# Zero products issued inside units, ahead of a product foreseen to wait, and a higher bound for those at units' ends

## The chip, the cores and the metric

One NeuronCore of a Trainium2 chip runs the whole kernel. The metric is the device time of one execution in microseconds; a lower one is better. In the profile, PE is the TensorE matmul, PEld its weight load, DVE the VectorE, ACT the ScalarE, POOL the GpSimd engine and SP the engine that issues DMAs.

## The reference

Four attention layers in a row, each with a layer norm before it and a residual added: A, B, A, B. There are 2048 tokens of width 512, and 32 heads of 16. Layer A cuts the sequence into 4 segments of 512, with causal attention inside each and a linear-attention memory carried from segment to segment; layer B is full attention without a mask.

```python
# layer A, for each of the 4 segments s
logits = jnp.einsum('bhqd,bhkd->bhqk', qs, ks) * scale + mask
p = _softmax(logits, axis=-1)
a_dot = jnp.einsum('bhqk,bhkd->bhqd', p, vs)
a_mem = num / den                      # phi(q) against the memory M, z
o = g * a_mem + (1.0 - g) * a_dot
# layer B
scores = jnp.einsum('bhqd,bhkd->bhqk', q, k) * Dh ** (-0.5)
p = _softmax(scores, axis=-1)
o = jnp.einsum('bhqk,bhkd->bhqd', p, v)
# the whole
x = x + _A_ref(_layernorm(x), ...); x = x + _B_ref(_layernorm(x), ...)   # twice
```

## The kernel before, in words

The work is cut into **units**. A unit takes up to three score banks: for three blocks of 128 keys of some head, TensorE multiplies keys by queries (`ps<-qm,KA`, `ps<-qm,KB` or `ps<-qm,QA`: K of 32 rows, so that four heads share the array, "row-shaped"), into PSUM. ACT turns them into exponentials `pT` (line 1644), two sets of banks taking turns. In layer A, POOL cuts the diagonal blocks to the causal half (line 1659). Two or three units later TensorE multiplies `pT` by the values into the **accumulator**, bank 7 (`ACC`). In one form the values stream through `pT` as weights (`ps<-VA,pT`, all 128 rows and columns, "full-shaped", 51 or 34 columns each); in the other (`ps<-pT,VB` and the like) `pT` streams through values of 17 columns ("narrow"). Each head's **group** has the accumulator to itself from its first value product to its last; then DVE divides by the row sums (`finish`). Some score blocks go to DVE and POOL, which work out the exponential by integer steps (`dxw`, lines 1185, 1255, 1300), to relieve ACT; their products read `dxw` or another tile that is free at that time. Projections of the neighbouring layers (`ps<-xT,wB`, `ps<-wA,xT`, `ps<-woB,oT` ...) are spread between the units.

The order of all this isn't written out: a planner (`Sched`) goes through the program once before it is built, adds each instruction to its engine's list, and estimates when it starts and ends (`estimate`; `t["pe"]` and `t["act"]` are the estimated times at which an engine is through with what it has). `attention` runs the loop over units; a table of numbers (`PIECES`) changes its rules as the estimated time goes by. Each engine works through its list in order and waits on semaphores only where the planner's dependencies ask for it.

**Zero products** are matmuls of a 128x128 tile of zeros (`zero`) by 512 columns of `wB`: they add zero, and are there to keep TensorE at work. `keep_busy` issues them at the end of each unit, into the open accumulator where the group has had a value product, else into bank 3. It has two rules. The first ("fill") enters its products into the planner's estimate. The second ("add") passes `extra`: `Sched.add` then leaves the estimate of every time as it is, and only notes the product in `true`, from which `worked` reads the share of a stretch of 3413 ns that TensorE's products fill. "add" goes on while this share, in the stretch that ends at the later of `t["pe"]` and `t["act"]` - 1330, is under `ADD`, to at most `ADDS` products in all.

Of the kernel before, what the change touches and what calls it, by code (L numbers as in the profile page):

```python
# [24 lines left out]
UNIT, DXB, ACC = (0, 4), 3, 7  # L25
# [3 lines left out]
LAG = {"pe": 100, "act": 60, "dve": 60, "pool": 70, "sp": 50}  # L29


class Op:
    __slots__ = ("eng", "idx", "fn", "deps", "emit", "evno", "is_dma", "batch", "name", "end")

    def __init__(self, eng, idx, fn, name=""):
        self.eng = eng
        self.idx = idx
        self.fn = fn
        self.deps = []
        self.emit = False  # L40
        self.evno = None
        self.is_dma = False
        self.batch = None
        self.name = name
        self.end = 0.0
# [35 lines left out]
class Sched:  # L81


    def __init__(self):
        self.ops = {e: [] for e in ENGS}
        self.t = {e: 0.0 for e in ENGS}
        self.tiles = []
        self.held = []

        self.streams = []  # L90
        self.true = []

    def streamed(self, until, ns):

        while self.streams and self.streams[0][0] < self.pe_issue() - 2 * ns:
            self.streams.pop(0)
        return sum(w for t, w in self.streams if t >= until - ns) / ns
# [47 lines left out]
    def add(self, eng, fn, reads=(), writes=(), deps=(), name="", banks=(), ns=300, gap=None, tile=None, extra=None):  # L145
        op = Op(eng, len(self.ops[eng]), fn, name)
        dep_ops = list(deps)
        for b in reads:
            if b.last_write is not None:
                dep_ops.append(b.last_write)  # L150
        for b in writes:
            if b.last_write is not None:
                dep_ops.append(b.last_write)
            dep_ops.extend(b.reads.values())
        for (bk, mode, alloc) in banks:
            if mode == "w":
                if bk.alloc != alloc:
                    tail = bk.writes[-1:] + list(bk.reads.values())
                    if not tail:
                        tail = list(bk.prev_tail)  # L160
                    dep_ops.extend(tail)
                    bk.prev_tail = tail
                    bk.alloc = alloc
                    bk.writes = []
                    bk.reads = {}
                    bk.last_read_any = None
                else:
                    dep_ops.extend(bk.reads.values())
                    if not bk.writes and not bk.reads:
                        dep_ops.extend(bk.prev_tail)  # L170
            else:
                assert bk.alloc == alloc, (bk.idx, bk.alloc, alloc, name)
                if bk.writes:
                    dep_ops.append(bk.writes[-1])
                else:
                    dep_ops.extend(bk.prev_tail)
                if bk.last_read_any is not None and bk.last_read_any.eng != eng:
                    dep_ops.append(bk.last_read_any)
        wit = {}
        for w in dep_ops:  # L180
            if w.eng == "pe" and eng == "pe" and not w.is_dma:
                continue
            if w.is_dma:
                wit[("dma", id(w.batch))] = w
                continue
            cur = wit.get(w.eng)
            if cur is None or cur.idx < w.idx:
                wit[w.eng] = w
        for w in wit.values():
            if not w.is_dma:  # L190
                w.emit = True
        op.deps = list(wit.values())
        if extra is not None:
            op.end = max([w.end for bk, mode, al in banks for w in bk.writes[-1:] or bk.prev_tail], default=0.0)
            self.true.append((extra, tile[5] / 2.4))
        else:
            self.estimate(op, ns, max(ns - 85, 60) if gap is None else gap, tile, name[:3] in ("dxs", "dxp"))
        for b in reads:
            b.reads[eng] = op
        for b in writes:  # L200
            b.last_write = op
            b.reads = {}
        for (bk, mode, alloc) in banks:
            if mode == "w":
                bk.writes.append(op)
            else:
                bk.reads[eng] = op
                bk.last_read_any = op
        self.ops[eng].append(op)
        return op  # L210
# [73 lines left out]
class Builder:  # L284
# [7 lines left out]
    DXA_N, DXA_W, APARTS, FILL_NEAR, FILL_FREE, HOR, PHI, QUAD = 13, ('k0', 'k13'), ('k2', 'k13', 'k0'), 0, 1, 400, 'kq', ('in', 1, 3)  # L292
    QREST, CLOSE, FM, NAREA, XDX, NEAR_S, NEAR_E, DX_WAIT = 24, ('proj', 2, 2), 3, 18, 99, 60, 60, 400
    DX_RES, CHAINS, ALT, ALTS, ALTA = 0, 4, 0, 3, (1, 1, 1, 1)
    PSH, PSH_N, PSH_B, PSH_E, TODO, ONE, MOST, FULLW, FULL_N, MIX, OPART, ADD, ADDS, ADD_A = 0, 12, 4, 0, 350, 0, 2, 1, 8, 0, 4, 0.5, 3, 1330
    ORDER = [[(-4.6, 7.7, 7.6, 0.9, -10), (3.8, -10.8, 0.4, 20, -10.8), (19, 59.6, 22, 59.8, 12), (31, 44.3, 46.9, 10.6, 0.2)],
             [(-1.5, -6.7, -5.8, 20.8, 1.2), (-5.2, -1.6, 28.5, 28, 7), (21, 35.0, 8.2, 30, 27.7), (21, 48.0, 37, 23.6, 12.2)]]
    PIECES = [(0.0, {'MIX': 0, 'OPART': 4}),
# [180 lines left out]
    def keep_busy(self):  # L479


        g, n = self.cur, 0
        own = g is not None and g.npv
        if not own and (self.bank_late() > 0 or any(t["next"][0][:1] == ["cont"] for t in self.tasks)):
            return
        bank, al = (self.banks[ACC], g.acc) if own else (self.banks[DXB], self.new_alloc())
        soon = [w.end + LAG[w.eng] for e in self.pvq[:9] if e[0] <= self.unit_no + 1 for w in (self.b_pT[e[4] * 3 + e[5]].last_write,)]
        at = max(self.sc.t["act"] - 1330, min(soon, default=0.0) - self.HOR)
        while n < self.FILLS and self.sc.streamed(max(self.sc.t["pe"], at), 3413) < self.FILL:
            self.mm(self.ps[:, bank.col0:bank.col0 + 512], self.zero[:, :], self.wB[:, 0, 0:512], not own, not own,  # L490
                    [self.b_zero, self.b_wB[0]], bank, al, "fill")
            n += 1
        at = max(self.sc.t["pe"], self.sc.t["act"] - self.ADD_A)
        while n < self.ADDS and self.sc.worked(at, 3413) < self.ADD:
            self.mm(self.ps[:, bank.col0:bank.col0 + 512], self.zero[:, :], self.wB[:, 0, 0:512], not own, not own,
                    [self.b_zero, self.b_wB[0]], bank, al, "add", extra=at - 1)
            n += 1

    def mm(self, out, lhsT, rhs, start, stop, reads, bank, alloc, name="", tile=(128, 0, 128, 0), n=512, on=None, extra=None):
# [1346 lines left out]
    def pv_close(self, g, must):  # L1846


        whole = lambda: g.npv == g.total and not any(t[1] is g for t in self.dxq) and not any(p["ents"][0][0] is g for p in self.pooled)
        if not whole():  # L1850
            self.pv_some(g, (), must)
            if must and any(p["ents"][0][0] is g for p in self.pooled):
                self.pool_feed(g)
                self.pv_some(g, (), True)
            while must and g.npv < g.total:
                self.forced += 1
                if any(e[0] is g for e in self.dx_build):
                    self.dx_close()
                if any(p["ents"][0][0] is g for p in self.pooled):
                    self.pool_feed(g)  # L1860
                    self.pv_some(g, (), True)
                    continue
                mine = [t for t, l in zip(self.dx_tasks, self.dx_now) if l and l[1][0][0] is g]
                self.forcing = True
                self.run(mine[0] if mine else self.dx_next())
                self.forcing = False
                self.pv_some(g, (), True)
            if not whole():
                return 0
        self.cur = self.pend = None  # L1870
        cost = self.finish(g)
        if g.last:
            self.nfin[(g.L, g.qseg)] = self.nfin.get((g.L, g.qseg), 0) + 1
            if self.nfin[(g.L, g.qseg)] == 8:
                self.flags.add(("attn", g.L, g.qseg))
        return cost
# [149 lines left out]
```

## Time and profile before

| what | value |
|---|---|
| median of 3 executions | 1755.17 us (1754.55 to 1759.04) |
| the profiled execution | 1755.03 us, its span 1753.0 us |
| busy: PE, ACT | 1586.9 us (91%), 1709.0 us (97%) |
| busy: DVE, POOL | 1489.3 us (85%), 650.2 us (37%) |
| mean granted TensorE clock | 0.998 |
| weight loads of `zero` | 190 |

The span runs from the first to the last instruction; the profiled execution's own time has 2.0 us more around it. Busy shares are means over stages with different limits, so the prediction reads single places: rows of the timeline have start, duration, engine, line, operation, tiles, shape and count, and in brackets the idle time before and what ended it. Neighbours of one kind are merged into one row with their count; a row's duration then runs from the first one's start to the last one's end. Nearly all products of TensorE are recorded on line 500, since the helper `mm` issues them.

### The profile page before, as it was taken

The numbers are of one execution on the slowest core, as the hardware profiler recorded it, in microseconds if no ns is written. First come the engines' busy times: TensorE is split into PE (matmuls) and PEld (weight loads), VectorE is DVE, ScalarE is ACT, GpSimd is POOL, SyncE is SP. The second block draws the span as 40 slices with busy tenths as digits, with TensorE's granted clock in tenths as the row PEclk, the third lists the DMA queues.
The fourth block names the chain that finished last, engine by engine and source line by source line (L and its number), as shares of the span: only waits on it lengthen the run. The fifth ranks groups of instructions, "written<-read, shape, count | busy, mean of one in ns | idle before, by whom it ended". The sixth has DMA issues, their size and how long they took to land.

```text
span 1753.0 us, 43708 instructions
## 1 busy us (share of the span) xinstructions
PE 1586.9 (91%) x17387; PEld 567.8 (32%) x17570; DVE 1489.3 (85%) x2912; ACT 1709.0 (97%) x1662; POOL 650.2 (37%) x1204
## 2 busy tenths in 40 slices
PE   7889898899898999989999989989899999999998
PEld 4445454453224222233222232242222222222222
DVE  6687867589986999887999879767999999999997
ACT  7999999999999999999999999999999999999998
POOL 4632415110016212234211252151155566666665
PEclk9999999999999999999999999999999999999999
DMA  6021101000001000010001010010000000000000
GB/s 175 20 48 31 32 17 26 14 12 5 13 1 26 1 1 13 13 20 8 13 8 23 10 23 16 13 26 13 1 13 1 2 7 8 1 1 13 1 1 13
DMA packets 86188, 30.08 MB, mean 17 GB/s; under 512 B 78816, under 2 KB 85472, under 8 KB 85984
## 3 DMA queue, kind: packets, MB, share of 16 engines
q1 hardware_dynamic: 85984, 27.29, 7.6%
q8 instruction: 137, 2.24, 0.6%
q14 instruction: 67, 0.55, 0.1%
HBM read 6.30 MB, written 2.10 MB: 5 GB/s over the span
## 4 chain that ended last, share of the span: by engine, by line
ACT 45%; PE 29%; issue 14%; DVE 9%; POOL 2%; DMA 1%; SPq 0%; ACTq 0%; DVEq 0%; POOLq 0%
ACT pT L1644 44%; PE ps L500 29%; POOL pT L1659 2%; DVE dxw L1185 1%; DMA xT<-xn 1%; DVE dxw L1255 1%; DVE QA L1185 1%; ACT amem L758 0%; DVE VA L1185 0%; DVE xT L1185 0%; DVE KB L1185 0%; DVE KA L1777 0%; DVE x L975 0%; DVE VB L538 0%; DVE lnst L643 0%
## 5 line engine op out<-in xcount | busy, mean ns | idle before, releaser
L1644 ACT ACTIVATE pT<-ps 128x1024 bf16<-128x1024 f32 (+4 forms) x1612 | 1677.2, 1184 | 29.3 <-PE ps L500 21.4
L500 PE MATMUL ps<-qm,KB 32*128 32x512 bf16 x3584 | 524.5, 385 | 68.1 <-ACT pT L1644 54.3
L500 PE MATMUL ps<-pT,VB 128*17 128x512 bf16 x2187 | 372.1, 385 | 9.7 <-ACT pT L1644 3.4
L1659 POOL TENSOR_SCALAR_AFFINE_SELECT pT<-pT 128x256 bf16<-128x256 bf16 (+2 forms) x523 | 212.3, 417 | 222.3 <-ACT pT L1644 209.4
L500 PEld LDWEIGHTS ps<-qm,KB 32*128 32x128 bf16 x3584 | 133.4, 91 | 462.8 <-ACT pT L1644 347.8
L1300 POOL TENSOR_TENSOR dxw<-dxw,dxc 128x256 int32<-128x256 int32 (+1 forms) x127 | 77.7, 614 | 391.3 <-DVE dxw L1185 76.2
L1185 DVE TENSOR_SCALAR dxw<-ps 128x512 uint16<-128x512 f32 (+1 forms) x232 | 158.5, 697 | 5.2 <-PE ps L500 4.2
L500 PEld LDWEIGHTS ps<-pT,VB 128*17 128x17 bf16 x2187 | 86.6, 87 | 233.3 <-issue 199.4
L1554 POOL TENSOR_SCALAR qm<-QB,par 128x512 bf16<-128x512 bf16 x88 | 67.4, 772 | 246.5 <-PE ps L500 221.7
L1185 DVE TENSOR_SCALAR QA<-ps 128x512 uint16<-128x512 f32 (+1 forms) x170 | 120.7, 729 | 5.2 <-PE ps L500 4.5
L500 PE MATMUL ps<-qm,KA 32*128 32x384 bf16 (+3 forms) x1024 | 101.5, 303 | 24.7 <-ACT pT L1644 19.8
L500 PE MATMUL ps<-qm,QA 32*128 32x512 bf16 x512 | 113.1, 384 | 11.7 <-ACT pT L1644 8.3
L500 PE MATMUL ps<-VA,pT 128*128 128x51 bf16 (+1 forms) x2560 | 107.1, 187 | 16.7 <-POOL pT L1659 8.2
L500 PE MATMUL ps<-dxw,VW 128*17 128x512 bf16 x472 | 117.9, 383 | 0.0
L1185 DVE TENSOR_SCALAR VA<-ps 128x512 uint16<-128x512 f32 (+1 forms) x149 | 107.1, 732 | 4.7 <-PE ps L500 3.7
L1255 DVE TENSOR_SCALAR dxw<-dxw 128x1024 uint16<-128x1024 uint16 (+1 forms) x261 | 104.8, 412 | 4.5 <-PE ps L500 2.3
L500 PEld LDWEIGHTS ps<-VA,pT 128*128 128x128 bf16 x2560 | 84.4, 96 | 64.3 <-POOL pT L1659 31.7
L1185 DVE TENSOR_SCALAR KB<-ps 128x512 uint16<-128x512 f32 (+1 forms) x122 | 93.8, 786 | 4.5 <-PE ps L500 3.5
L500 PE MATMUL ps<-dxw,VB 128*17 128x512 bf16 x297 | 89.5, 382 | 0.1
L1185 DVE TENSOR_SCALAR VB<-ps 128x512 uint16<-128x512 f32 (+1 forms) x106 | 82.7, 794 | 3.6 <-PE ps L500 2.5
L500 PE MATMUL ps<-pT,VA 128*17 128x512 bf16 x367 | 74.7, 384 | 1.3 <-ACT pT L1644 1.1
L500 PE MATMUL ps<-VB,pT 128*128 128x34 bf16 (+1 forms) x1788 | 69.3, 186 | 2.0 <-ACT pT L1644 1.1
(343 smaller groups left out, 2782.9 us busy)
## 6 DMA issues: line engine op xcount, KB each, us to landing
out_dram<-x SPq DMA_DIRECT2D x8, 256.0 KB, 2.2
x<-in_A_x_dram SPq DMA_DIRECT2D x3, 512.0 KB, 5.1
wB<-in_B_wqkv_dram SPq DMA_DIRECT2D x1, 1536.0 KB, 11.8
xT<-xn SPq DMA_TRANSPOSE x60, 2.4
oT<-ob SPq DMA_TRANSPOSE x36, 2.4
x<-in_A_x_dram SPq DMA_DIRECT2D x4, 128.0 KB, 2.4
wA<-in_A_wq_dram SPq DMA_DIRECT2D x1, 512.0 KB, 4.5
wA<-in_A_wk_dram SPq DMA_DIRECT2D x1, 512.0 KB, 5.9
```

The source lines that it names most:

```text
L500: self.sc.add("pe", lambda e: e.matmul(out, lhsT, rhs, start=start, stop=stop, skip_group_check=True), reads=reads, banks=[(bank, "w", all ...
L1185: self.sc.add("dve", lambda e: e.tensor_scalar(d, o, SCALE * LOG2E * 128, W_C if dxs[0][:3] in self.wt else EXP_C, op0=ALU.mult, op1=ALU.add),
L1255: self.op("dve", lambda e: e.tensor_scalar(o, w, d, None, op0=ALU.add), reads=self.b_dxw[b0][:len(ents)], writes=wr, ns=(295, 425, 560, 69 ...
L1300: self.sc.add("pool", lambda e: e.tensor_tensor(o, w, c, ALU.add), reads=self.b_dxw[src][i0:i0 + n] + [self.b_dxc], writes=wr, deps=[sync] ...
L1554: self.op(eng, (lambda m, q, col: lambda e: e.tensor_scalar(m, q, col, 0.0, op0=ALU.mult, op1=ALU.add))(m, q, col), reads=[bq, self.b_par] ...
L1644: self.sc.add("act", (lambda dst, src: lambda e: e.activation(dst, src, ACT.Exp, scale=SCALE))(dst, src), writes=self.b_pT[slot * 3 + i:sl ...
L1659: self.op("pool", (lambda blk, pat: lambda e: e.affine_select(blk, blk, pattern=pat, compare_op=ALU.is_ge, fill=0.0, base=0, channel_multi ...
```

## The change

`Sched.add` gets a hook, `idle`. When an instruction of TensorE is added that depends on another engine, and the latest of those dependencies (its estimated end, and `LAG` for the semaphore) is more than 312 ns after `t["pe"]`, it first calls the hook. The hook, `keep_idle_busy`, issues zero products into the open accumulator, each counted as 226 ns, while the next one is still more than 312 ns ahead of the foreseen time and the share of work in the 3413 ns up to it is under `ADD`, at most `ADDI` = 4 of them. It does so only if the accumulator belongs to a group that has had value products, has some left, and hasn't been read. As with "add", the planner's times don't move. `ADD` goes from 0.5 to 0.55, for `keep_busy` too.

```diff
@@ Sched.add
         op.deps = list(wit.values())
+        if eng == "pe" and extra is None and self.idle is not None:
+            ready = max([d.end + LAG[d.eng] for d in op.deps if d.eng != "pe"], default=0.0)
+            if ready > self.t["pe"] + 312:
+                self.idle(ready, banks)
+                op.idx = len(self.ops[eng])
@@ Builder
-    ... MIX, OPART, ADD, ADDS, ADD_A = 0, 12, 4, 0, 350, 0, 2, 1, 8, 0, 4, 0.5, 3, 1330
+    ... MIX, OPART, ADD, ADDS, ADD_A, ADDI = 0, 12, 4, 0, 350, 0, 2, 1, 8, 0, 4, 0.55, 3, 1330, 4
+    def keep_idle_busy(self, ready, banks):
+
+        g, bank, n = self.cur, self.banks[ACC], 0
+        if g is None or not g.npv or not g.left or bank.alloc != g.acc or not bank.writes or bank.reads:
+            return
+        at = self.sc.t["pe"]
+        while n < self.ADDI and at + 312 < ready and self.sc.worked(ready, 3413) < self.ADD:
+            self.mm(self.ps[:, bank.col0:bank.col0 + 512], self.zero[:, :], self.wB[:, 0, 0:512], False, False,
+                    [self.b_zero, self.b_wB[0]], bank, g.acc, "add", extra=at)
+            at += 226
+            n += 1
@@ pv_close
         self.cur = self.pend = None
+        self.sc.idle = self.keep_idle_busy
         cost = self.finish(g)
```

In the built program TensorE's list has 329 zero products where it had 190. The lists of all other engines, and the order and the waits of the rest, are the same. At three places, on TensorE, in rows of line, operation, out<-in, shape and count (the changed kernel's line is 518, and a row with a wait names the semaphores that it waits for, `ev_` and an engine):

Near 102 us of the trace, between the first layer A and the first layer B, where the first scores of B (`qm,KB`) wait for DVE. Before:

```order
L500 MATMUL ps<-VA,pT 128x3x17 x5
L500 MATMUL ps<-wB,xT 128x512 [waits ev_act]
L500 MATMUL ps<-wB,xT 128x512 x3
L500 MATMUL ps<-qm,KB 128x512 [waits ev_dve]
L500 MATMUL ps<-qm,KB 128x512 x2
L500 MATMUL ps<-xT,wB 128x512 x4
```

Now:

```order
L518 MATMUL ps<-VA,pT 128x3x17 x5
L518 MATMUL ps<-wB,zero 128x512
L518 MATMUL ps<-wB,xT 128x512 [waits ev_act]
L518 MATMUL ps<-wB,xT 128x512 x3
L518 MATMUL ps<-wB,zero 128x512 x3
L518 MATMUL ps<-qm,KB 128x512 [waits ev_dve]
L518 MATMUL ps<-qm,KB 128x512 x2
L518 MATMUL ps<-xT,wB 128x512 x4
```

One zero product has come in front of the projection `wB,xT` that waits for ACT, and three in front of the scores that wait for DVE.

Near 535 us, in the second layer A, where a unit ends and the next one's scores (`qm,KA`) wait for ACT. Before:

```order
L500 MATMUL ps<-qm,KA 128x256 [waits ev_act]
L500 MATMUL ps<-qm,KA 128x256 x2
L500 MATMUL ps<-VA,pT 128x3x17 [waits ev_pool]
L500 MATMUL ps<-VA,pT 128x3x17 x11
L500 MATMUL ps<-qm,KA 128x384 [waits ev_act]
L500 MATMUL ps<-qm,KA 128x384
```

Now:

```order
L518 MATMUL ps<-qm,KA 128x256 [waits ev_act]
L518 MATMUL ps<-qm,KA 128x256 x2
L518 MATMUL ps<-VA,pT 128x3x17 [waits ev_pool]
L518 MATMUL ps<-VA,pT 128x3x17 x11
L518 MATMUL ps<-wB,zero 128x512
L518 MATMUL ps<-qm,KA 128x384 [waits ev_act]
L518 MATMUL ps<-qm,KA 128x384
```

A zero product has come between twelve value products and the scores.

Near 1728 us, at the end of layer B, between scores and narrow value products (tiles such as `KB` and `wA`, free by then, hold exponentials from DVE and values). Before:

```order
L500 MATMUL ps<-KB,VW 17x512 x2
L500 MATMUL ps<-qm,KB 128x512 [waits ev_act]
L500 MATMUL ps<-qm,KB 128x512 x2
L500 MATMUL ps<-KB,wA 17x512
L500 MATMUL ps<-dxw,wA 17x512 x2
```

Now:

```order
L518 MATMUL ps<-KB,VW 17x512 x2
L518 MATMUL ps<-qm,KB 128x512 [waits ev_act]
L518 MATMUL ps<-qm,KB 128x512 x2
L518 MATMUL ps<-wB,zero 128x512
L518 MATMUL ps<-KB,wA 17x512
L518 MATMUL ps<-dxw,wA 17x512 x2
```

Here it has come between the scores and the first narrow product, which waits for no other engine.

More of the change, by code (lines that the diff above doesn't have):

```diff
@@ L91, in __init__ @@
         self.true = []
+        self.idle = None
     def streamed(self, until, ns):
@@ L294 @@
     DX_RES, CHAINS, ALT, ALTS, ALTA = 0, 4, 0, 3, (1, 1, 1, 1)
-    PSH, PSH_N, PSH_B, PSH_E, TODO, ONE, MOST, FULLW, FULL_N, MIX, OPART, ADD, ADDS, ADD_A = 0, 12, 4, 0, 350, 0, 2, 1, 8, 0, 4, 0.5, 3, 1330
+    PSH, PSH_N, PSH_B, PSH_E, TODO, ONE, MOST, FULLW, FULL_N, MIX, OPART, ADD, ADDS, ADD_A, ADDI = 0, 12, 4, 0, 350, 0, 2, 1, 8, 0, 4, 0.55, 3, 1330, 4
     ORDER = [[(-4.6, 7.7, 7.6, 0.9, -10), (3.8, -10.8, 0.4, 20, -10.8), (19, 59.6, 22, 59.8, 12), (31, 44.3, 46.9, 10.6, 0.2)],
```

## The prediction

> **What bounds the kernel now.** I read the page first: busy shares, the chain that ended last, then the groups of the two engines it names.
>
> ```profile
> span 1753.0 us, 43708 instructions
> PE 1586.9 (91%) x17387; PEld 567.8 (32%) x17570; DVE 1489.3 (85%) x2912; ACT 1709.0 (97%) x1662; POOL 650.2 (37%) x1204
> ACT 45%; PE 29%; issue 14%; DVE 9%; POOL 2%; DMA 1%; SPq 0%; ACTq 0%; DVEq 0%; POOLq 0%
> ...
> L1644 ACT ACTIVATE pT<-ps 128x1024 bf16<-128x1024 f32 (+4 forms) x1612 | 1677.2, 1184 | 29.3 <-PE ps L500 21.4
> L500 PE MATMUL ps<-qm,KB 32*128 32x512 bf16 x3584 | 524.5, 385 | 68.1 <-ACT pT L1644 54.3
> ...
> L500 PE MATMUL ps<-VA,pT 128*128 128x51 bf16 (+1 forms) x2560 | 107.1, 187 | 16.7 <-POOL pT L1659 8.2
> ```
>
> ScalarE's exponentials (ACT, L1644) set the pace: busy for 97% of the span, and idle ahead of them for 29.3 us in all, 21.4 of it waiting for TensorE's scores. TensorE (PE) is second. It waits for ACT ahead of the score products, but the chain still runs through PE for 29% of the span, and for another 14% as "issue", where nothing in the profile is waited for. So PE has slack in many places and none in others, and ACT can regain little once it is late.
>
> Then the granted clock. The page's row of 20 us slices shows it under full speed twice before the end, and the table by stretches, cut finely there, gives this:
>
> ```profile
> core 0: us, PE busy (x) PEld busy (x) DVE busy (x) ACT busy (x) POOL busy (x), PEclk, DMA share, GB/s
> 39.14:42.55 3.41, 1.61 (x25) 0.78 (x24) 2.53 (x6) 3.09 (x3) 1.00 (x4) 1.00 0.19 38
> 42.55:45.96 3.41, 3.41 (x24) 1.24 (x22) 0.69 (x1) 3.26 (x5) 1.83 (x5) 0.50 0.00 0
> ...
> 585.27:588.68 3.41, 2.57 (x27) 0.60 (x25) 3.27 (x7) 3.41 (x5) 0.92 (x2) 1.00 0.00 0
> 588.68:592.10 3.42, 2.95 (x20) 0.63 (x22) 1.68 (x4) 1.92 (x3) 0.00 (x0) 0.50 0.00 0
> ...
> 1189.40:1192.80 3.40, 2.23 (x20) 0.68 (x20) 3.19 (x11) 3.40 (x3) 0.69 (x1) 1.00 0.02 5
> ```
>
> Two stretches of 3.41 us ran at half clock, each behind a stretch in which PE was less busy than usual. What they cost is what ACT then waited for PE (its timeline):
>
> ```profile
> 47.52 2.79 ACT L1644 ACTIVATE pT<-ps 128x1536 bf16<-128x1536 f32 x2 [1.24 <-PE ps L500]
> ...
> 590.46 1.02 ACT L1644 ACTIVATE pT<-ps 128x1024 bf16<-128x1024 f32 x1 [1.02 <-PE ps L500]
> 591.96 4.76 ACT L1644 ACTIVATE pT<-ps 128x1024 bf16<-128x1024 f32 x5 [0.48 <-PE ps L500]
> ```
>
> That is 1.24 us for the first and 1.02 + 0.48 = 1.50 us for the second, 2.74 us together. This is all that a steadier clock can return of this execution.
>
> **What moves.** In the built program TensorE gets 329 zero products where it had 190; every other instruction of every engine, and each one's order, is unchanged. No DMA moves. Of the 177 that the two "add" rules place (38 before), 58 come from the new rule inside units and 119 from the old rule at units' ends. Compared place by place, 144 are new (58 inside, 86 at ends) and 5 old ones at ends are gone. One wait moves: the first zero product that needs `wB` now stands earlier.
>
> ```profile
> 11.17 0.70 SPq L569 DMA_DIRECT2D wB<-in_B_wqkv_dram  x1
> ...
> wB<-in_B_wqkv_dram SPq DMA_DIRECT2D x1, 1536.0 KB, 11.8
> ...
> 30.86 0.28 PE L500 MATMUL ps<-qm,KA 32*128 32x256 bf16 x3 [0.27 <-ACT pT L1644]
> ```
>
> That load has landed by 11.17 + 11.8 = 23 us, and the first new zero product stands in front of the scores of 30.86, so this costs nothing.
>
> **What a zero product costs where nothing covers it.** Two places of TensorE's timeline: a zero product that the kernel already has, ahead of row-shaped scores, and a place without one.
>
> ```profile
> 183.56 0.36 PE L500 MATMUL ps<-VA,pT 128*128 128x51 bf16 x8 [0.82 <-POOL pT L1659]
> 183.77 0.38 PE L500 MATMUL ps<-wB,zero 128*128 128x512 bf16 x1
> 184.07 0.28 PE L500 MATMUL ps<-qm,KA 32*128 32x256 bf16 x3
> ...
> 534.56 0.49 PE L500 MATMUL ps<-VA,pT 128*128 128x51 bf16 x12
> 534.98 0.39 PE L500 MATMUL ps<-qm,KA 32*128 32x384 bf16 x6
> ```
>
> The scores follow a zero product's start by 0.30 us (184.07 - 183.77). Twelve value products took 0.49 us, one takes 0.19 (187 ns above), so they start 0.027 apart: the last starts at 534.86, the scores 0.12 us later, with no wait. A zero product between them would start 0.03 after that last one, and the scores 0.30 behind it: 0.33 in place of 0.12, so 0.21 us more. Next to products that write 17 columns ("narrow") it is dearer, because it stands between two changes of shape:
>
> ```profile
> 627.43 0.39 PE L500 MATMUL ps<-qm,KB 32*128 32x512 bf16 x3 [0.21 <-ACT pT L1644]
> 627.76 1.04 PE L500 MATMUL ps<-woB,oT 128*128 128x512 bf16 x4
> 628.72 0.39 PE L500 MATMUL ps<-pT,VB 128*17 128x512 bf16 x2
> ...
> 1728.22 0.39 PE L500 MATMUL ps<-qm,KB 32*128 32x512 bf16 x3 [0.16 <-ACT pT L1644]
> 1728.54 0.38 PE L500 MATMUL ps<-KB,wA 128*17 128x512 bf16 x1
> ```
>
> Scores to a full-shaped product took 0.33 us (627.76 - 627.43). The four full-shaped ones end 1.04 - 0.38 = 0.66 us after their first start with the last one's start, 628.42; the narrow product follows 0.30 later. Scores straight to a narrow product took 0.32 (1728.54 - 1728.22). So a zero product there adds 0.33 + 0.30 - 0.32 = 0.31 us.
>
> **How many are covered.** I set each of the 144 against the gap that the trace shows at its place. The first with a wide gap, and its neighbours:
>
> ```profile
> 100.35 1.04 PE L500 MATMUL ps<-wB,xT 128*128 128x512 bf16 x4
> ...
> 102.65 0.39 PE L500 MATMUL ps<-qm,KB 32*128 32x512 bf16 x3 [1.26 <-DVE qm L1554]
> ```
>
> Three new zero products stand here in 1.26 us of idle time (and the pipeline's tail before it): covered. At 534.98 there is no wait, and one costs 0.21 us. From the first uncovered place, in the value products that start at 74.14, to the last, at 1728.54, the count is:
>
> ```profile
> 74.14 0.79 PE L500 MATMUL ps<-VA,pT 128*128 128x51 bf16 x24
> ```
>
> - 51 covered in full (37 of them inside units): 0 us;
> - 31 where the wait is too short by under 0.12 us, 0.03 us on average: 1.1 us;
> - 62 with little or no wait: 47 of them cost 9.7 us (0.21 each), 15 next to narrow products or in pairs 3.8 us: 13.4 us with rounding. 54 of the 62 stand at units' ends, and only 2 are of the inside rule alone.
>
> So TensorE is held up by 14.5 us in all. The rule at ends looks at how little work was done, not at whether PE will wait; that is why it is the dear one. The 5 removed ones give back at most 5 x 0.21 = 1.1 us, and I leave them out.
>
> **What reaches the end.** Between nothing (each delay taken up by the next wait for ACT, 54.3 us of those in the scores' row) and all 14.5. The nearest row is the chain: a delay of PE lies on it where the chain runs through PE, 29%, or PE and issue, 43%. ACT's spare 29.3 us is small, so a little more stays: I take half, 7.25 us.
>
> **What comes back.** One new zero product stands in each of the two stretches ahead of the half clock:
>
> ```profile
> 41.91 0.28 PE L500 MATMUL ps<-qm,KA 32*128 32x256 bf16 x3 [1.80 <-ACT pT L1644]
> ...
> 588.36 0.38 PE L500 MATMUL ps<-qm,KB 32*128 32x512 bf16 x1 [0.31 <-DVE VA L1185]
> ```
>
> The second stretch was busy for 2.57 of 3.41 us and comes nearer to its neighbours; I count its half clock as gone, 1.50 us. The first was busy for 1.61, and one product does little against a wait of 1.80; I leave it. The bounds are 0 and 2.74 us.
>
> Sum: 1755.03 (the profiled execution: 1753.0 and 2.0 around it, 0.1 under the median of three) + 7.25 - 1.50 = 1760.8 us.
>
> [...]
>
> **The rivals.**
> 1. *Covered after all, faster.* ACT's queue of scores takes up each delay, and both half-clock stretches go: 1755.03 - 2.74 = 1752.3 us. For it: 54.3 us of PE's waits for ACT. Against it: the chain's 43%. It decides once under 2.74 / 14.5 = 19% of the delays land. Unprofiled executions may hold more half-clock stretches: the highest of the three, 1759.04, is 4.0 us above the profiled one, about three more at 1.37 each; if that is common before and gone after, the same 1752.3 us is over 0.3% faster.
> 2. *Everything lands.* PE paces the loop of scores, exponentials, values wherever it does not wait: 1755.03 + 14.5 = 1769.5 us. Against it: the waits that follow.
> 3. *The zero products do nothing for the clock.* PE was busy for 2.23 us at 1189.40, less than in 585.27, and the clock stayed full behind it; busy time alone does not decide. Then only the cost stays: 1755.03 + 7.25 = 1762.3 us. [...]
>
> **How the numbers follow.** 0.3%, about what a measurement of this kernel can tell from no change, is 5.3 us: 1749.9 and 1760.4. The forecast, 0.52, has its own range of 1756.6 to 1764.5 (30% of the delays landing and both stretches gone, 1755.03 + 4.35 - 2.74; 65% and none gone, 1755.03 + 9.4) and lies on the slow side of the bound for 0.32 and within for 0.20. Rival 1: 0.24, half faster, half within. Rival 2: 0.14, slower. Rival 3: 0.10, 0.06 slower and 0.04 within. Slower 0.52, same 0.36, faster 0.12. The range holds the forecast's own, rival 3, most of rival 1 and the nearer part of rival 2: 1752.5 to 1766.0.
>
> **What would show it.** Right: 329 weight loads of `zero`; ACT's wait for PE above 21.4 us; the scores at 534.98 and the narrow product at 1728.54 later behind their forerunners by 0.21 and 0.31 us; full clock near 588 us. Wrong: ACT's idle time unchanged or less (rival 1), half-clock stretches as before (rival 3), or PE's share of the chain far above 29% (rival 2).

## The result: 0.6% slower

| kernel | median | runs | range |
|---|---|---|---|
| before | 1754.85 us | 6 | 1753.73 to 1759.04 |
| after | 1765.42 us | 6 | 1763.26 to 1766.89 |

After over before is 1.0058, with a 95% interval of 1.0045 to 1.0071: 10.6 us longer, past the bound of 0.3%. The forecast was 1760.8 us and its range reached to 1766.0. The profiled execution took 1766.89 us, the slowest of the six; its span is 11.4 us above that of before (1764.4 and 1753.0).

The same lines of the page as in the prediction, now of the kernel after:

```profile
span 1764.4 us, 43959 instructions
...
PE 1613.0 (91%) x17499; PEld 577.2 (33%) x17709; DVE 1491.6 (85%) x2912; ACT 1711.8 (97%) x1662; POOL 649.2 (37%) x1204
...
ACT 42%; PE 34%; issue 13%; DVE 9%; POOL 2%; DMA 1%; SPq 0%; ACTq 0%; DVEq 0%; POOLq 0%
...
L1662 ACT ACTIVATE pT<-ps 128x1024 bf16<-128x1024 f32 (+4 forms) x1612 | 1679.9, 1182 | 37.5 <-PE ps L518 30.2
L518 PE MATMUL ps<-qm,KB 32*128 32x512 bf16 x3584 | 523.4, 385 | 62.3 <-ACT pT L1662 49.2
```

TensorE's share of the chain rose from 29% to 34%. Its waits for ACT ahead of the scores fell from 54.3 to 49.2 us: by that row, only 5.1 us of the added work went into waits. The exponentials account for nearly all of the difference: idle ahead of them 37.5 instead of 29.3 us (+8.2), and busy 1679.9 instead of 1677.2 us (+2.7), together 10.9 of the 11.4 us.

Why they were busy for longer: 1612 of 1184 ns would be 1908.6 us, but the group was busy for 1677.2, since one exponential overlaps the next where ACT doesn't stop, by 0.14 us on average. The table of waits shows how often it stopped (us in total, times, longest). Before:

```profile
ACT pT L1644 <- PE ps L500: 21.4, 56, 1.2
```

After:

```profile
ACT pT L1662 <- PE ps L518: 30.2, 78, 2.2
```

22 stops more, at 0.14 us of overlap each, are an estimated 3.1 us, about the 2.7 above. The agreement is rough, because the exponentials themselves also became shorter (1182 ns on average instead of 1184, 3.2 us over 1612). By this estimate a late score block costs ACT the wait and the overlap.

The three places of the prediction in TensorE's timeline after:

```profile
99.72 1.04 PE L518 MATMUL ps<-wB,xT 128*128 128x512 bf16 x4
100.60 0.81 PE L518 MATMUL ps<-wB,zero 128*128 128x512 bf16 x3
102.03 0.39 PE L518 MATMUL ps<-qm,KB 32*128 32x512 bf16 x3 [0.62 <-DVE qm L1572]
...
536.28 0.49 PE L518 MATMUL ps<-VA,pT 128*128 128x51 bf16 x12
536.60 0.38 PE L518 MATMUL ps<-wB,zero 128*128 128x512 bf16 x1
536.91 0.39 PE L518 MATMUL ps<-qm,KA 32*128 32x384 bf16 x6
...
1739.46 0.39 PE L518 MATMUL ps<-qm,KB 32*128 32x512 bf16 x3 [0.16 <-ACT pT L1662]
1740.11 0.38 PE L518 MATMUL ps<-KB,wA 128*17 128x512 bf16 x1 [0.25 <-issue]
```

At the first, the scores come 2.31 us after the first projection product; before it was 2.30. The three zero products cost nothing. At the second, scores follow the first value product by 0.63 instead of 0.42 us: 0.21 more. At the third, scores to narrow product took 0.65 instead of 0.32 us: 0.33 more. The zero product itself is missing from the matmul records there (246 of 329 are recorded); the weight loads have all:

```profile
L518 PEld LDWEIGHTS ps<-wB,zero x329: 95/96/147, 30.7 to 1739.8; 128*128 128x128 bf16 x165
```

The same rows locate the loss: the kernel after is 0.63 us ahead at the first (99.72 against 100.35), 1.72 behind at the second and 11.24 behind at the third.

The clock's stretches after, and the place near 588 us:

```profile
core 0: us, PE busy (x) PEld busy (x) DVE busy (x) ACT busy (x) POOL busy (x), PEclk, DMA share, GB/s
588.68:592.10 3.42, 2.89 (x29) 0.76 (x26) 3.23 (x7) 3.33 (x5) 0.53 (x1) 1.00 0.00 0
...
1034.53:1037.94 3.41, 1.94 (x37) 0.96 (x36) 2.95 (x7) 3.41 (x5) 1.59 (x3) 1.00 0.00 0
1037.94:1041.35 3.41, 3.19 (x16) 1.13 (x17) 1.04 (x3) 1.26 (x3) 1.62 (x5) 0.50 0.54 45
1580.66:1584.07 3.41, 2.82 (x24) 0.72 (x22) 3.34 (x7) 3.41 (x5) 2.56 (x5) 1.00 0.00 0
1584.07:1587.49 3.42, 3.42 (x23) 0.54 (x22) 3.17 (x5) 2.94 (x4) 1.93 (x4) 0.50 0.02 5
```

Full clock near 588 us, as foretold, and near 42 us too. But two other stretches ran at half clock, at 1037.94 and 1584.07. Neither of these two gains can be credited to the new zero products. Near 42 us TensorE's wait still stands after the change; what differs is where the stretches of 3.41 us begin, so that two of them share it, with PE busy for 2.65 and 2.48 us where one was busy for 1.61 before:

```profile
42.18 0.28 PE L518 MATMUL ps<-qm,KA 32*128 32x256 bf16 x3 [1.53 <-ACT pT L1662]
...
37.84:41.25 3.41, 2.65 (x39) 1.24 (x35) 2.06 (x6) 2.71 (x4) 1.56 (x4) 1.00 0.17 33
41.25:44.66 3.41, 2.48 (x36) 1.30 (x37) 2.15 (x5) 3.41 (x4) 2.01 (x5) 1.00 0.05 10
```

Near 588 us the same scores with the same wait ran at full clock in the kernel without the "add" products (below), which has no zero product between 580 and 600 us:

```profile
591.64 0.39 PE L511 MATMUL ps<-qm,KB 32*128 32x512 bf16 x1 [0.31 <-DVE VA L1196]
...
589.00:592.42 3.42, 2.58 (x28) 0.68 (x24) 3.35 (x7) 3.42 (x5) 0.48 (x1) 1.00 0.00 0
592.42:595.83 3.41, 3.41 (x35) 0.83 (x32) 3.25 (x6) 3.36 (x5) 0.25 (x1) 1.00 0.00 0
```

What ACT waited at the two new stretches, after:

```profile
1041.42 0.60 ACT L1662 ACTIVATE pT<-ps 128x512 bf16<-128x512 f32 x1 [2.21 <-PE ps L518]
...
1585.92 2.10 ACT L1662 ACTIVATE pT<-ps 128x1024 bf16<-128x1024 f32 x2 [0.43 <-PE ps L518]
1588.49 1.45 ACT L1662 ACTIVATE pT<-ps 128x1536 bf16<-128x1536 f32 x1 [0.46 <-PE ps L518]
```

The exponential of 1041.42 had waited for 0.44 us before:

```profile
1034.32 1.60 ACT L1644 ACTIVATE pT<-ps 128x512 bf16<-128x512 f32 x3 [0.44 <-PE ps L500]
```

So the waits at the two new stretches grew by 1.77 + 0.89 = 2.7 us, and those at the two that went were worth 2.74. (Some 0.4 us of the 1.77 belong to a second zero product that the change puts there: its weight load follows that of the first by 0.42 us, at half clock.) In this pair of executions the clock gave next to nothing; about all of the 11.4 us are the price of the zero products.

### The profile page after: what moved, and what is told of

It is laid out like the page before. It is cut to its first block, busy times and chain, and to the rows that moved or that the text cites. A ratio compares the mean times of both kernels' runs of the same rounds, so it can differ in the third digit from the quotient of the medians.

```text
span 1764.4 us, 43959 instructions
## 1 busy us (share of the span) xinstructions
PE 1613.0 (91%) x17499; PEld 577.2 (33%) x17709; DVE 1491.6 (85%) x2912; ACT 1711.8 (97%) x1662; POOL 649.2 (37%) x1204
## 4 chain that ended last, share of the span: by engine, by line
ACT 42%; PE 34%; issue 13%; DVE 9%; POOL 2%; DMA 1%; SPq 0%; ACTq 0%; DVEq 0%; POOLq 0%
ACT pT L1662 41%; PE ps L518 34%; POOL pT L1677 2%; DVE KB L1203 1%; DMA xT<-xn 1%; DVE QA L1203 1%; ACT amem L776 0%; DVE KA L1795 0%; DVE dxw L1203 0%; DVE dxw L1273 0%; DVE xT L1203 0%; DVE phq L1203 0%; DVE VB L1203 0%; DVE x L993 0%; DVE ob L1777 0%
## 5 line engine op out<-in xcount | busy, mean ns | idle before, releaser
L1662 ACT ACTIVATE pT<-ps 128x1024 bf16<-128x1024 f32 (+4 forms) x1612 | 1679.9, 1182 | 37.5 <-PE ps L518 30.2
L518 PE MATMUL ps<-qm,KB 32*128 32x512 bf16 x3584 | 523.4, 385 | 62.3 <-ACT pT L1662 49.2
L518 PE MATMUL ps<-wB,zero 128*128 128x512 bf16 x246 | 80.0, 382 | 4.2 <-issue 3.0
```

What stands on the lines that cost most here:

```text
L518: self.sc.add("pe", lambda e: e.matmul(out, lhsT, rhs, start=start, stop=stop, skip_group_check=True), reads=reads, banks=[(bank, "w", all ...
L1662: self.sc.add("act", (lambda dst, src: lambda e: e.activation(dst, src, ACT.Exp, scale=SCALE))(dst, src), writes=self.b_pT[slot * 3 + i:sl ...
```

## The experiments

The theories: **A** is the prediction's, that a zero product costs by its place: nothing where a wait covers it, 0.2 to 0.3 us of TensorE's time where none does, part of which lands. **B**: each of the 139 added costs the same, 10.6 / 139 = 0.076 us, wherever it stands. **C**: the price is the change of shape and the weight load, not the 512 columns. All zero products add zero to an accumulator, so no kernel below leaves out any part of the result. Each was timed in alternation with the kernel before on one chip; kernels that share a figure for before ran together. Two more theories stand in the expectations: **D**, that the short waits are no cover at all, and **E**, that the zero products hold the clock.

### The two rules apart

The rule inside units alone (223 zero products: 33 more than before), and the higher bound at ends alone (294):

```diff
-... ADD, ADDS, ADD_A, ADDI = ... 0.55, 3, 1330, 4
+... ADD, ADDS, ADD_A, ADDI = ... 0.5, 3, 1330, 4      # inside only
+... ADD, ADDS, ADD_A, ADDI = ... 0.55, 3, 1330, 0     # ends only
```

> Only the rule inside units: ADD back at 0.5, ADDI 4. TensorE gets 223 zero products, 33 more than before; set against the gaps in the trace of before, 28 of the 36 at new places are covered in full, and the others hold TensorE up by 0.7 us in all. Theory A (a zero product costs only what the wait at its place does not cover, and about 0.75 of that, 10.6 us over 14.5, reaches the end): 0.5 us over before, 1755.4 us, and not over 1756.5. Theory B (each zero product costs the same, 10.6 us / 139 = 0.076 us, by being issued, loaded and written): 33 x 0.076 = 2.5 us over before, 1757.4 us.

> Only the higher bound at units' ends: ADD 0.55, ADDI 0. 294 zero products, 104 more than before and 35 fewer than the whole change. Against the gaps in the trace of before, 14 are covered in full, 24 nearly (0.8 us in all) and 74 not (16.8 us). Theory A (uncovered delay times 0.75): 17.6 x 0.75 = 13.2 us over before, 1768.1 us, slower than the whole change with its 139. Theory B (0.076 us each): 104 x 0.076 = 7.9 us over before, 1762.8 us, faster than the whole change.

### The new zero products sorted by cover

Of the 144 new places, those of one class of the prediction's count keep theirs, and the others lose it. `LIMIT` holds, by place in TensorE's list, how many stay; the planner's record of work keeps all, so nothing else moves:

```diff
@@ Sched.add
+        if eng == "pe" and extra is not None:
+            self.here += 1
+            if self.here > LIMIT.get(self.real, 99):
+                self.true.append((extra, tile[5] / 2.4))
+                return None
...
+        if eng == "pe" and extra is None:
+            self.real, self.here = self.real + 1, 0
```

> The whole change, but of its 144 new places only the 51 zero products that the trace of before covers in full are issued; the 93 others are left out, each place given by its number in TensorE's list. 236 zero products, 46 more than before. Theory A: nothing is held up, so before's time within 1 us, 1753.9 to 1755.9 us. Theory B: 46 x 0.076 = 3.5 us over before, 1758.4 us.

> The whole change, but of its 144 new places only the 62 zero products with little or no wait in the trace of before are issued. 247 zero products, 57 more than before, 11 more than in the kernel with the covered ones. Theory A: 13.4 us of delay times 0.75, 10 us over before, 1764.9 us, nearly the whole change's cost. Theory B: 57 x 0.076 = 4.3 us over before, 1759.2 us.

> The whole change, but of its 144 new places only the 31 zero products are issued for which the wait in the trace of before is too short by under 0.12 us, 1.1 us of delay in all. 216 zero products, 26 more than before. Theory A: 1.1 x 0.65 = 0.7 us over before, 1755.4 us. Theory D (the whole change's last 2.5 us, over the 8.1 of the uncovered ones alone, come from these, since a wait that ACT ends is no slack for ACT): 2 to 3 us over before, 1757.2 us.

### Shorter zero products

The 144 new ones stream 128 columns instead of 512:

```diff
+            if self.here > LIMIT.get(self.real, 99):
+                fn = short
...
+                    short=lambda e: e.matmul(out[:, 0:128], lhsT, rhs[:, 0:128], start=start, stop=stop, skip_group_check=True))
```

> The whole change, but each of the 144 zero products at new places streams 128 columns where it had 512; number and places are the same, and the old ones stay at 512. Theory A (uncovered delay): each holds TensorE 0.16 us (384 columns at 2.4 per ns) less, so the delays against the trace of before fall from 14.5 to 3.8 us; with 0.65 of a delay reaching the end (0.60 to 0.73 in the runs so far) 2.5 us over before, 1757.2 us. Theory C (the two changes of shape around a zero product, and its weight load, are the cost, not its length): as the whole change, 1765 us.

What these six measured:

| kernel | zero products | median | before | ratio (95%) |
|---|---|---|---|---|
| inside only | 223 | 1754.38 | 1754.69 | 0.9997 (0.9988 to 1.0006) |
| ends only | 294 | 1765.74 | 1754.69 | 1.0065 (1.0052 to 1.0077) |
| 51 covered only | 236 | 1755.01 | 1754.69 | 0.9998 (0.9989 to 1.0007) |
| 62 uncovered only | 247 | 1762.76 | 1754.69 | 1.0045 (1.0032 to 1.0057) |
| 31 short waits only | 216 | 1756.81 | 1755.07 | 1.0009 (1.0001 to 1.0018) |
| 144 new ones short | 329 | 1758.78 | 1755.07 | 1.0022 (1.0012 to 1.0033) |

A and B part on the third and fourth. Their pages (span, chain, exponentials), the uncovered alone first:

```profile
span 1760.7 us, 44005 instructions
...
ACT 43%; PE 34%; issue 13%; DVE 7%; POOL 2%; DMA 1%; SPq 0%; ACTq 0%; DVEq 0%; POOLq 0%
...
L1678 ACT ACTIVATE pT<-ps 128x1024 bf16<-128x1024 f32 (+4 forms) x1612 | 1678.8, 1182 | 34.8 <-PE ps L534 25.2
```

The covered alone:

```profile
span 1753.1 us, 43983 instructions
...
ACT 45%; PE 29%; issue 13%; DVE 10%; POOL 2%; DMA 1%; SPq 0%; ACTq 0%; DVEq 0%; POOLq 0%
...
L1679 ACT ACTIVATE pT<-ps 128x1024 bf16<-128x1024 f32 (+4 forms) x1612 | 1677.2, 1187 | 28.9 <-PE ps L535 21.0
```

B falls: 46 more zero products in covered places cost nothing, 57 more in uncovered ones 8.1 us, where B had 3.5 and 4.3. The uncovered bring back the 34% of the chain and most of the idle time and of the lost overlap (1678.8 us busy, 34.8 idle); the covered leave these numbers close to those of before. The ends-only kernel, with 35 zero products fewer than the whole change, is as slow as it, and the inside rule alone is free: the loss belongs to the rule at ends. A's sizes were less good: the ends-only kernel costs 11.0 us (9.1 to 13.5) where A had 13.2, and the uncovered ones 8.1 (5.6 to 10.0) where it had 10. Cover and rule go together for the most part, since 54 of the 62 uncovered places are at ends and 37 of the 51 covered ones inside; that 14 covered places at ends were free with the others speaks for cover.

C falls in the main: with a quarter of the columns (such a product is recorded with 219 ns, one of 512 columns with 379) and all the shape changes and weight loads, the change costs 3.7 instead of 10.6 us. That is 1.2 us above the 2.5 us that A gave, but the interval (2.1 to 5.8 us) holds both, so whether shape and load cost something besides the length is not shown.

The short waits cost 1.7 us, between A's 0.7 and the 2 to 3 us of D; the interval (0.2 to 3.2 us) rules out neither. The class may have been sized too small: the waits that the trace showed are of one execution, and a place counted as 0.03 us short may be shorter in the next. No run shows that.

### What zero products do for the clock

The kernel before without the 38 of its "add" rule, and without all 190. The planner's times stay, and the instructions keep their order:

```diff
+LEFT_OUT = ('add',)            # the second kernel: ('add', 'fill')
...
+            if op.name in LEFT_OUT:
+                continue
```

> The kernel before, its order kept, without the 38 zero products of its second rule at units' ends; the 152 of the first rule stay. Theory A: most of them stand where TensorE does not wait either: 2.7 us of delay at places of their own and up to 4 in places shared with the first rule, times 0.65: 1.8 to 4.4 us faster than before, 1750.3 to 1752.9 us. Theory E (they hold the clock): half-clock stretches, 1.37 us each, come in their place; with 3 more the gain is gone, 1754.7 us or above, and the mean granted clock falls from 0.998 to 0.995.

> The kernel before, its order kept, without any of its 190 zero products. Theory A: against the pipeline's spacing in the trace of before they hold TensorE up by 24.6 us; times 0.65, 16 us faster than before, 1738.7 us, if the clock stays. Theory E (they hold the clock): each half-clock stretch costs 1.37 us, so 12 more of them, a mean granted clock of 0.987, eat the gain up; with more it is slower than before, over 1755 us.

Without the 38: 1758.02 against 1755.07 us, 1.0012 (1.0004 to 1.0021). Without all: 1770.02 us, 1.0088 (1.0072 to 1.0105). The page of the kernel without any, the clock in slices and the exponentials:

```profile
PEclk9889999999997999999999999988999999999999
...
L1655 ACT ACTIVATE pT<-ps 128x1024 bf16<-128x1024 f32 (+4 forms) x1612 | 1678.7, 1184 | 42.2 <-PE ps L511 35.5
```

And its table by stretches:

```profile
core 0: us, PE busy (x) PEld busy (x) DVE busy (x) ACT busy (x) POOL busy (x), PEclk, DMA share, GB/s
0.00:100.00 100.00, 84.99 (x1054) 45.20 (x1055) 61.49 (x168) 82.53 (x97) 52.34 (x140) 0.88 0.36 95
400.00:1000.00 600.00, 553.39 (x5276) 171.12 (x5272) 537.09 (x1073) 589.40 (x597) 140.21 (x275) 0.97 0.06 11
```

The granted clock is 0.97 over 600 us in which PE was busy for 92%. So E holds, and A by itself, which had both kernels faster than before (1750.3 to 1752.9 and 1738.7 us), does not: without zero products the clock is lower (0.9713 in the mean of the runs, 0.9980 before), and it is so though TensorE is busy for 91% of the span.

How much each set of them holds shows in all runs together. Each run has its time and its mean granted clock; a straight line through the runs of one kernel gives its time at full clock (for the first row, whose runs lie between 0.966 and 0.975, this reaches far beyond them, and the standard error from the scatter of its runs is some 7 us; for the second and fourth it is 1.4 and 0.9 us, for the third 0.2):

| kernel | zero products | mean clock | time at full clock |
|---|---|---|---|
| none | 0 | 0.9713 | 1743.8 us |
| without "add" | 152 | 0.9939 | 1750.8 us |
| before | 190 | 0.9980 | 1752.7 us |
| after | 329 | 0.9988 | 1764.1 us |

On these lines 0.001 of clock less is 0.9 to 1.3 us more, and 0.001 is about one stretch of 3.41 us at half clock (3.41 x 0.5 / 1753). By the lines the first 190 zero products cost 8.9 us at full clock and save some 24 us of half clock (1770.02 - 1743.8 = 26.2 us without them, 2.4 with). Both sizes move with the 7 us of the first row; their difference, 15 us between the medians, is measured. The 139 that the change adds cost 11.4 us by the lines and raise the clock by 0.0008, about 1 us: what was left to save was 0.0020, some 2 to 3 us.

### Zero products only where the planner foresees a wait

The inside rule with a margin of 420 ns instead of 312 and a share of 0.8 instead of `ADD`, beside the old rule at ends (285 zero products), and in its place (250):

```diff
-            if ready > self.t["pe"] + 312:
+            if ready > self.t["pe"] + 420:
-        while n < self.ADDI and at + 312 < ready and self.sc.worked(ready, 3413) < self.ADD:
+        while n < self.ADDI and at + 420 < ready and self.sc.worked(ready, 3413) < 0.8:
-... ADD, ADDS, ADD_A, ADDI = ... 0.55, 3, 1330, 4
+... ADD, ADDS, ADD_A, ADDI = ... 0.5, 3, 1330, 4      # beside the rule at ends
+... ADD, ADDS, ADD_A, ADDI = ... 0.0, 3, 1330, 4      # in its place
```

> An attempt at a faster version. The ends keep their bound of 0.5; the rule inside units asks for 420 ns of foreseen wait in place of 312, and goes on to a share of 0.8. 285 zero products; of the 98 at new places 90 are covered in full, the rest hold TensorE up by 0.6 us. By delay and clock together (0.65 of a delay lands; 1.14 us for each 0.001 of clock): 0.4 us of cost, and a clock of 0.999 to 1.000 in place of 0.998 gives 1 to 2 us back: 1753.3 to 1754.3 us, 0.5 to 1.5 us faster than before. If products inside units do nothing for the clock: 1755.4 us.

> As the last, but with no zero products by the second rule at units' ends at all (ADD 0): 250 zero products, 98 by the rule inside units (35 places at ends are gone). By delay and clock together: the kernel without the second rule would take 1750.8 us at full clock, by the line through its runs; 0.4 us for the inside ones; a clock of 0.997 to 0.999 adds 1.1 to 3.4: 1752.3 to 1754.6 us. If products inside units do nothing for the clock (0.994): 1758 us.

The last kernel is the second of these without those 85 of the 152 "fill" products that no wait covers (165 zero products stay):

> As the last, but of the first rule's 152 zero products at units' ends the 85 are left out that the trace of before does not cover, the plan kept: 165 zero products. By delay and clock together: without any zero products the line through the runs gives 1743.8 us at full clock; covered ones add 1 us at most; the clock decides: at 0.995 5.7 us more, 1750.5 us; at 0.990 1756.2 us; break-even with before at 0.991. If covered ones do as much for the clock as the uncovered ones, 165 in place of 152 (0.994 without the second rule) give 0.994 or more and 1751.6 us or less.

| kernel | zero products | median | before | ratio (95%) | mean clock | at full clock |
|---|---|---|---|---|---|---|
| beside | 285 | 1755.55 | 1755.24 | 1.0001 (0.9992 to 1.0010) | 0.9985 | 1753.3 us |
| in its place | 250 | 1751.89 | 1755.24 | 0.9982 (0.9972 to 0.9992) | 0.9984 | 1750.5 us |
| uncovered fills out | 165 | 1755.97 | 1755.24 | 1.0005 (0.9996 to 1.0013) | 0.9910 | 1748.9 us |

The second is faster than before by 0.2% (the interval lies below 1), and so faster than the change. Its page:

```profile
span 1748.4 us, 43803 instructions
...
ACT 45%; PE 29%; issue 14%; DVE 9%; POOL 2%; DMA 1%; SPq 0%; ACTq 0%; DVEq 0%; POOLq 0%
...
L1662 ACT ACTIVATE pT<-ps 128x1024 bf16<-128x1024 f32 (+4 forms) x1612 | 1676.7, 1185 | 25.2 <-PE ps L518 17.4
```

ACT waits for PE for 17.4 us instead of 21.4; some 2.7 of these 4 us are the waits behind the two half-clock stretches of the execution before, which this execution (clock 1.000) did not have. At full clock the kernel stands at the 1750.8 us of the kernel without "add": its 98 inside products cost nothing, and hold the clock at 0.9984 where that one had 0.9939. The first was expected to be faster by 0.5 to 1.5 us and is not: it keeps 35 products at ends and their cost, and the clock was nearly full already. The third leaves 85 uncovered products out. At full clock that may gain 1.6 us, which is no more than the standard error of its line (1.4 us), and the clock takes more: its 165 products, 98 of them inside, hold the clock at 0.9910, where the 152 fills alone held 0.9939. So covered ones do not replace the fills.

## Why the prediction was right, and where its sizes were off

- **The direction and its cause: right.** The change pays TensorE's time for a clock that was nearly full. 329 weight loads and more than 21.4 us of waits (30.2) came as written. Full clock near 588 us came too, but it is no sign of the mechanism: the kernel without the "add" products shows it as well.
- **What a zero product costs: right.** 0.21 us measured for 0.21 at the second place, 0.33 for 0.31 at the third.
- **How many are covered: right as a sorting.** The covered class costs nothing, the uncovered 8.1 us, and the rule at ends is the dear one. The short class measured 1.7 us instead of a part of 1.1; the interval (0.2 to 3.2 us) holds both.
- **What reaches the end: mis-sized.** Half of 14.5, 7.25 us, was taken; 11.4 / 14.5 = 79% landed (with the covered and short classes' small parts in it). For the uncovered alone it was 8.1 / 13.4 = 60%. The half was a choice a little above the chain's 43%, without a working of what a delay does to ACT; the pages show 8.2 us more idle time (57%) and, which the term left out, 2.7 us of busy time from lost overlap. The three classes by themselves give 0.3 + 8.1 + 1.7 = 10.1 of the 10.6 us between the medians.
- **What comes back: wrong.** The half clock at 588 us went as foretold, and the one at 42 us as well, but two others came elsewhere: 0 instead of 1.50 us in the profiled pair, about 1 us over all runs. The step took the stretches of one execution for properties of the program alone. They are not: over its runs of up to 1759.4 us the clock of the kernel before varied from 0.995 to 1.000 with the program unchanged. Near 42 us the two traces show what goes with it: before, a stretch of 3.41 us begins 39.14 us after the start and holds all of TensorE's wait of 1.80 us (busy for 1.61 us); after, a boundary of these stretches, at 41.25 us, lies inside the wait of 1.53 us, and the two that share it are busy for 2.65 and 2.48 us. So the full clock that the kernel after has at both places can't be credited to the change; in this pair it was at least in part luck. (The step also named the wrong view: the page's own row has slices of 43.8 us, all at 9; the stretches came from a finer table.)

These two errors, 4 us and 1.5 us, go the same way and make 5.6 of the 6.1 us by which the sum fell short of the profiled execution. The median, 1765.42, lies above the forecast's own range (to 1764.5) and in the part that was added for rival 2, 0.6 us under the upper end.

- **Rival 1, covered after all: refuted for the change** (it needed under 19% of the delays to land), but true of the inside rule, which alone is free.
- **Rival 2, everything lands: nearer than I had it.** 1765.42 lies 4.1 us under its 1769.5, and 4.6 above the forecast.
- **Rival 3, zero products do nothing for the clock: refuted** by the runs with 0 and 152 of them (mean clock 0.9713 and 0.9939, where 190 had 0.9980), though for the 139 added here it was nearly so in its sum: two stretches at half clock before the end in both executions, as its sign said, and its 1762.3 us are nearer than the forecast. In the stretches ahead of the half clock PE was busy for 1.61 and 2.57 us before and for 1.94 and 2.82 us after, of 3.41 us.

**Left open:** what decides whether the clock is halved behind a stretch, since it stayed full behind one that was busy for 2.23 us before (from 1189.40 us), and behind one of 1.81 us after (from 89.04 us). The three classes at full clock (7.5 + 1.7 + 0.5 = 9.7) also fall 1.7 us short of the whole (11.4), but the lines have standard errors of up to 0.9 us each, so that may be noise; between the medians 0.5 us is missing.

## What to carry to other kernels

Work that is meant to fill a second engine's idle time belongs ahead of waits that the trace shows, not wherever the load looks low: zero products of the same kind were free in covered places (46 of them: 0.3 us), and about 60% of their time reached the end in the others (8.1 of 13.4 us). Price a delay of the pacing engine's supplier as the wait and the lost overlap of two of its instructions (here 8.2 and 2.7 us). And before buying a resource, work out what is left to buy: here 0.2% of the clock.

## What the runs showed of the hardware

In the traces of before and after the clock stood at half (PEclk 0.50) for 3.41 us at a time, in stretches on a grid of that length: the two of before (42.55 and 588.68) and the two of after (1037.94 and 1584.07) are both 546.13 us apart, 160 stretches. The distance is not always 160: in the trace of before the clock is at half once more from 1752.63 us, 0.37 us before the span's end and 341 stretches after 588.68. The grid does not start with the kernel: counted back from the first half clock, a stretch begins 39.14 us after the start in the trace of before, and 37.84 and 41.25 in that of after. By the lines through the runs each stretch at half clock costs this kernel, in which ACT is busy for 97% of the span, an estimated 0.9 to 1.3 us of the 1.7 that it is short of (3.41 x 0.5). A full-shaped product of 512 columns ahead of one of another shape took 0.30 us to the next start (183.77 to 184.07 before), against 0.22 between neighbours of its own shape (1.04 - 0.38 = 0.66 us for three).
